# Filling TensorE's planned gaps with identity products during the first two attention units

## Chip, cores and metric

The kernel runs on one core of one Trainium2 chip. The metric is the device time of one execution in microseconds (us), from the first to the last thing that the core does. Lower is better.

## What is computed

Three stages follow one another. The first is an attention through packed queries: 32 packed queries per head attend to the 576 keys of their head, and the 576 true queries then attend to the 32 results. The second is a feed-forward layer with a gated activation. The third mixes 8 experts, whose weights per token come from a softmax that is normalised 8 times over rows and columns.

```python
p_packed = sm_attn(p, k, v)              # 4 batches, 8 heads, 32 packed queries, 64 wide
x = sm_attn(q, p_packed, p_packed)       # 2304 tokens x 512
h = x @ w_in; g = h * clip(h + 3, 0, 6) / 6; x = g @ w_out
P = softmax-like(x @ w_gate), normalised 8 times
out = sum over e of P[:, e] * (relu(x @ w1[e]) @ w2[e])
```

## The kernel before, in words

The attention is cut into 8 units `u` (a batch and four of its heads each), written by `attention(u, p_sb)`. A unit loads k, the packed queries p, q and v by DMA, and then on TensorE (PE): transposes k (L553, twelve transposes into `kT`), transposes the packed queries (L570), multiplies them with `kT` (L595, the first scores), transposes q (L643, nine), transposes the exponentials (L663, six), multiplies with v (L679), transposes the result (L704), multiplies with the transposed q (L736, the second scores), and transposes the second exponentials (L794, L798). Between these steps ScalarE (ACT), VectorE (DVE) and GpSimd (POOL) copy results out of PSUM, take maxima, exponentials and sums. The buffers of k, q, v and `kT` are single, so the DMA of a unit's k waits until the unit before has transposed its own.

Beside the attention, the feed-forward weights, which come as 64-bit floats, are decoded by integer and float operations on ACT, DVE and POOL (`split_f64`, L344 to L369) into `w1f` and others. Then the dense layers follow (L837, L886 to L888, L924 to L926, then L992 to L994 and L1050 to L1052), which start as soon as their operands are there.

The order is made by a planner, the class `Order`. Every operation is entered with an engine, a cost in microseconds, the buffers that it reads, writes or takes, and a priority. `run` keeps a clock per engine and again and again picks the open operation with the earliest planned start; what is picked is issued at once, by calling its function. The engines then work in that order, each strictly through its own queue, and the real waits are semaphores. The planned times decide the order alone. The costs that matter below are these:

```python
SYNC = 0.2                                            # added between an operation and what follows on it
def dma(kib, fn, **kw):                               # queue SP
    return order.op([("SP", max(0.6, kib / 350.0), fn)], lat=2.0, **kw)
pe(0.25, trans, reads=[kp[g]], writes=[ps], ...)      # three transposes of k, L553; four such steps in a unit
pe(0.55, scores, ...)                                 # half of the first scores, L595
pe(0.11 * n, trans, reads=[qp], ...)                  # n transposes of q, L643
pe(1.55, packed, ...)                                 # L679
pe(0.15 * len(tiles), scores, ...)                    # second scores, L736; 9 tiles in two steps
```

The queue SP is planned to issue two pieces of weights (512 KB each), four pieces of k (entered with 288), the first packed queries (64), four pieces of q (288) and v (576), in this order, and then the next pieces of weights and the next unit's k. `psum("po")` gives a bank of 128x512 floats; the two banks of that tag are used by the dense layers (L924 onward), not by the attention. `ident` is the 128x128 identity in 32-bit floats, made by POOL at the start.

Of the kernel before, what the change touches and what calls it, by code (L numbers as in the profile page):

```python
# [27 lines left out]
class Res:  # L28


    def __init__(self, count):
        self.free_at = [0.0] * count
# [31 lines left out]
class Order:  # L64
# [2 lines left out]

    def __init__(self):
        self.open, self.clock, self.all = [], {}, []

    def op(self, ways, reads=(), writes=(), fills=(), takes=(), after=(), prio=0, lat=0.0):
        deps = set(after)
        for h in (*reads, *writes):
            deps.update(h.writers)
        for h in writes:
            deps.update(h.readers)
        holds = list(dict.fromkeys((*reads, *writes, *fills, *takes)))
        for h in holds:
            h.users += 1
        o = Op(ways, holds, deps, (prio, len(self.all)), lat)  # L80
        self.all.append(o)
        for h in reads:
            h.readers.append(o)
        for h in (*writes, *fills):
            h.writers.append(o)
        if not o.wait:
            self.open.append(o)
        return o

    def run(self):  # L90
        while self.open:
            best = None
            for o in self.open:
                at, asked = o.ready, {}
                for h in o.holds:
                    if h.slot is None:
                        asked[h.res] = asked.get(h.res, 0) + 1
                for r, n in asked.items():
                    free = sorted(r.free_at)
                    at = max(at, free[n - 1] if len(free) >= n else float("inf"))  # L100
                _, start, eng, cost, fn = min(
                    (
                        (max(at, self.clock.get(w[0], 0.0)) + sum(w[3:], w[1]), max(at, self.clock.get(w[0], 0.0)), *w[:3])
                        for w in o.ways
                    ),
                    key=lambda w: w[0],
                )
                key = (start + PATIENCE * (o.lat == 0 and (o.prio[0] >= 100 or 9 < o.prio[0] < 20 and o.prio[0] % 1 > 0.3)), o.prio)
                if best is None or key < best[0]:
                    best = (key, start, o, eng, cost, fn)  # L110
            _, start, o, eng, cost, fn = best
            assert start < float("inf"), "no operation can go on"
            for h in o.holds:
                if h.slot is None:
                    h.slot = min(range(len(h.res.free_at)), key=lambda i: h.res.free_at[i])
                    h.res.free_at[h.slot] = float("inf")
                    h.t = h.make(h.slot)
            self.clock[eng] = self.now = start + cost
            fn()
            self.open.remove(o)  # L120
            o.end = start + cost + o.lat
            for h in o.holds:
                h.users -= 1
                h.last = max(h.last, o.end)
                if h.users == 0:
                    h.res.free_at[h.slot] = h.last + SYNC
            for a in o.after:
                a.wait.discard(o)
                a.ready = max(a.ready, o.end + SYNC)
                if not a.wait:  # L130
                    self.open.append(a)
# [19 lines left out]
def tile_kernel(  # L151
# [16 lines left out]
    nc = tc.nc  # L168
# [4 lines left out]
    E, _, F2 = moe2_w1.shape  # L173
# [82 lines left out]
    ident = const.tile([128, 128], F32, name="ident")  # L256
# [6 lines left out]
    order = Order()  # L263

    def maker(tag, shape, dt, parts):
        def make(i):
            r = res[tag]
            pool = r.pool if i < r.first else r.late_pool if i < r.first + r.late or not r.late else r.last_pool
            got = [pool.tile(shape, dt, tag=f"{tag}{x}_{i}", name=f"{tag}{x}_{i}") for x in parts]
            return got if len(parts) > 1 else got[0]  # L270

        return make

    def hold(tag, shape, dt=F32):
        return Hold(res[tag], maker(tag, shape, dt, ("",)))
# [544 lines left out]
    def psum(tag):  # L820
        return hold(tag, [128, 512])
# [381 lines left out]
    def early(gg):  # L1203

        return (9.4, 9.4, 13.4, 14.4, 100, 100, 100, 100)[gg]

    with tc.manual_schedule():
        nc.vector.memset(ones, 1.0)
        nc.vector.memset(three, 3.0)
        nc.vector.memset(maskb, 0.0)  # L1210
        nc.vector.memset(maskb[0:64, 0, :], 1.0)
        nc.vector.memset(maskb[64:128, 1, :], 1.0)
        nc.vector.memset(maskz, 0.0)
        for g in range(2):
            for h in range(2):
                r0 = 64 * g + 32 * h
                nc.vector.memset(maskz[r0:r0 + 32, g, h, :], 1.0)

        place("p0", att, 1)
        place("p1", att, 1)  # L1220
        p_sb = hold("p0", [128, 1, D]), hold("p1", [128, NU - 1, D])
        for u in range(NU):
            attention(u, p_sb)
        ws, pws = {}, {}

        def weights(gg):
            prio, soon = early(gg), gg < 4
            ws[gg] = (
                whole(gg, "w1", prio, "w1f", soon),
                whole(gg, "w2", prio + 0.5, ("w2", "w2o")[gg % 2], soon),  # L1230
            )

        for gg in range(4):
            weights(gg)
        order.op([("", 0.0, second_phase)], after=order.all)

        gps(0.2, lambda: nc.gpsimd.memset(wg.t, 0.0), writes=[wg], prio=90)
        dma(
            16,
            lambda: nc.sync.dma_start(wg.t[:, :, :E], moe2_w_gate.rearrange("(c p) e -> p c e", p=128)),  # L1240
            writes=[wg], prio=90,
        )
        begun = len(order.all)
        for i, (blk, g) in enumerate(units):
            batches = [span[0] for span in spans(blk)]
            for gg in (2 * g, 2 * g + 1):
                if gg not in ws:
                    weights(gg)
            for b in batches:
                if (b, 2 * g) not in pws:  # L1250
                    ggs = (2 * g, 2 * g + 1)
                    for some in [ggs] if i >= TOGETHER else [ggs[:1], ggs[1:]]:
                        pws.update(zip(((b, gg) for gg in some), packed_weights(i, b, [ws[gg][0] for gg in some])))
            hs = [pair("hs", [128, NFC, TB]) for _ in range(2)]
            for f in range(2 * NFC):
                layer1a(i, blk, f, {b: pws[b, 2 * g + f // NFC] for b in batches}, hs[f // NFC])
            layer2a(i, g, blk, [ws[2 * g][1], ws[2 * g + 1][1]], hs)
        uses = [[o for o in order.all[begun:] if a2[b] in o.holds] for b in range(B)]
        freed = []
        for b, count in enumerate((1, 2, 1, 2)):  # L1260
            freed = [order.op([("", 0.0, first_operands(count))], after=[*uses[b], *freed])]
        order.op([("", 0.0, third_phase)], after=order.all[begun:])
        for blk in range(NB):
            gate(blk)
        ops = {0: operands(0, 40)}
        routing()
        i = len(units)
        turn, done = 100 + G1, []
        for ps in passes:
            for pr in ps:  # L1270
                if pr not in ops:
                    ops[pr] = operands(
                        pr, 45 if pr > 1 else 200, lambda n, pr=pr: [done[-1] if pr > 1 else done[4 + 3 * n]]
                    )
            gs = list(range(G1, len(groups)))
            turns_of = [(gs[:2], pr) for pr in ps] + [([g], pr) for g in gs[2:] for pr in ps]
            ready = {}
            for some, pr in turns_of:
                for g in some:
                    if g not in ready:  # L1280
                        ready[g] = (*combined(g, turn), whole(g, "w2", turn, "w2"))
                        turn += 1
                for g in some:
                    wa, wb, w2 = ready[g]
                    hs = [pair("hs", [128, NFC, TB]) for _ in range(2)]
                    done.append(layer1b(i, ops[pr], wa, wb, hs))
                    for h in range(2):
                        layer2b(i, g, 2 * pr + h, w2, hs[h])
                    i += 1
        order.run()  # L1290
# [32 lines left out]
```

## Time and profile before

| | us |
|---|---|
| median of 3 runs | 1956.97 (1956.45 to 1958.83) |
| the profiled execution | 1956.3 |
| its span, first to last instruction | 1954.5 |
| TensorE busy in the span | 1917.1 |
| VectorE, ScalarE, GpSimd busy | 1216.6, 971.5, 887.5 |

The profile's times count from the first instruction of the span. The profiled execution lasts 1.8 us longer than its span and is 0.7 us under the median of the runs. A matrix product is two instructions, a load of the stationary operand (PEld) and a stream of the moving one (PE); the two rows overlap. A product of 32-bit floats that is not a transpose is issued as two such pairs. In a line of the timeline the columns are start, duration from the first start to the last end, engine, line of the code, operation, tiles written and read, shape, how many instructions, and in brackets the idle time of the engine before them with what ended it. "PEclk" is the clock that TensorE was granted as a share of 2.4 GHz, as far as the profile recorded it.

### The profile page before, as it was taken

The page shows a single profiled execution, that of the slowest core. Times are in us where ns is not written, and L with a number is a line of the kernel's source. Part 1 is how long each engine was busy: PE and PEld are TensorE (multiplying, and loading weights), DVE is VectorE, ACT ScalarE, POOL GpSimd, SP SyncE. Part 2 cuts the span into 40 slices and gives each one's busy share as a digit, 9 for nine tenths or more (in the row PEclk, how much of TensorE's full clock was granted, in tenths as well). Part 3 has the DMA queues.
Part 4 walks back from the last instruction along what each step waited for, and adds up shares of the span by engine and source line. Part 5 has one row for each costly group of instructions (what it writes and reads, how often), then busy time and mean ns, then how long its engine had stood idle before and what let it go on. Part 6 is the DMA issues. An engine that isn't in the chain of part 4 may idle for free.

```text
span 1954.5 us, 28065 instructions
## 1 busy us (share of the span) xinstructions
PE 1917.1 (98%) x10573; PEld 1736.5 (89%) x10573; DVE 1216.6 (62%) x2010; ACT 971.5 (50%) x2185; POOL 887.5 (45%) x925
## 2 busy tenths in 40 slices
PE   6999999999999999999999999999999999999998
PEld 4789999998899999999899999999999999999997
DVE  6996686447876766666745655555555555555554
ACT  6885674335455555555654443444444344444432
POOL 2445675246755666555633533334343342433321
PEclk9999999999999999999999999999999999999999
DMA  9831121001222222222311101111010111101102
GB/s 212 190 91 33 53 67 44 11 1 44 66 65 73 68 66 67 74 65 66 86 33 32 44 22 44 33 33 41 25 44 24 42 33 33 44 22 44 33 12 65
DMA packets 103544, 104.85 MB, mean 54 GB/s; under 512 B 42736, under 2 KB 78576, under 8 KB 103408
## 3 DMA queue, kind: packets, MB, share of 16 engines
q1 hardware_dynamic: 103408, 103.06, 19.2%
q8 instruction: 83, 1.36, 0.3%
q14 instruction: 53, 0.43, 0.1%
HBM read 98.32 MB, written 4.72 MB: 53 GB/s over the span
## 4 chain that ended last, share of the span: by engine, by line
PE 89%; DVE 7%; ACT 2%; issue 1%; POOL 0%; DMA 0%; SPq 0%; DVEq 0%; ACTq 0%; POOLq 0%
PE po L1052 13%; PE po L1051 13%; PE po L1050 13%; PE ph L992 12%; PE ph L994 12%; PE ph L993 12%; PE po L924 3%; PE po L926 3%; PE po L925 3%; PE ph L886 2%; PE ph L888 1%; PE ph L887 1%; PE ph L837 1%; DVE m_early L344 0%; DVE tmp L904 0%
## 5 line engine op out<-in xcount | busy, mean ns | idle before, releaser
L429 POOL TENSOR_TENSOR hsl<-tmp,hsh 128x384 fp32r<-128x384 f32 x382 | 389.9, 1028 | 812.1 <-PE ph L994 482.4
L1074 DVE SCALAR_TENSOR_TENSOR acc<-po,Pr,acc 128x512 f32<-128x512 f32 x504 | 372.4, 747 | 286.4 <-PE po L1052 285.9
L1052 PE MATMUL po<-w2h,hsl 128*128 128x512 f32 x1152 | 448.7, 389 | 0.3 <-DVE hsl L429 0.3
L1050 PE MATMUL po<-w2h,hsh 128*128 128x512 f32 x1152 | 449.0, 390 | 0.0
L1051 PE MATMUL po<-w2l,hsh 128*128 128x512 f32 x1152 | 448.7, 390 | 0.0
L300 ACT ACTIVATE tmp<-ph 128x384 f32<-128x384 f32 x291 | 141.4, 486 | 402.7 <-PE ph L994 401.1
L1006 DVE TENSOR_TENSOR tmp<-ph,tmp 128x384 f32<-128x384 f32 x288 | 159.2, 553 | 270.9 <-PE ph L994 184.2
L1052 PEld LDWEIGHTS po<-w2h,hsl 128*128 128x128 f32 x1152 | 216.2, 188 | 45.9 <-DVE hsl L429 0.8
L1050 PEld LDWEIGHTS po<-w2h,hsh 128*128 128x128 f32 x1152 | 216.3, 188 | 41.6
L1051 PEld LDWEIGHTS po<-w2l,hsh 128*128 128x128 f32 x1152 | 216.3, 188 | 41.6
L424 ACT ACTIVATE hsh<-tmp 128x384 fp32r<-128x384 f32 x480 | 239.3, 519 | 18.5 <-DVE tmp L904 12.5
L424 ACT ACTIVATE w2h<-raw 128x1024 fp32r<-128x1024 f32 x64 | 68.1, 1064 | 327.2 <-PE po L1052 315.1
L1014 ACT ACTIVATE tmp<-tmp 128x384 f32<-128x384 f32 x288 | 149.8, 520 | 36.2 <-DVE tmp L1006 29.5
L429 POOL TENSOR_TENSOR w1l<-raw,w1h 128x512 fp32r<-128x512 f32 (+1 forms) x124 | 157.2, 1268 | 0.2 <-ACT w1h L424 0.2
L992 PE MATMUL ph<-ax,w1h 128*128 128x384 f32 x448 | 151.2, 338 | 0.6 <-DVE tmp L301 0.6
L994 PE MATMUL ph<-ax,w1l 128*128 128x384 f32 x448 | 150.7, 336 | 0.0
L993 PE MATMUL ph<-ax,w1h 128*128 128x384 f32 x448 | 150.5, 336 | 0.0
L992 PE MATMUL ph<-xyh,w1h 128*128 128x384 f32 x320 | 108.1, 338 | 3.0 <-ACT tmp L300 3.0
L994 PE MATMUL ph<-xyh,w1l 128*128 128x384 f32 x320 | 108.0, 338 | 0.0
L993 PE MATMUL ph<-xyl,w1h 128*128 128x384 f32 x320 | 107.9, 337 | 0.0
L994 PE MATMUL ph<-ax,w1xl 128*128 128x384 f32 x320 | 107.8, 337 | 0.0
L992 PE MATMUL ph<-ax,w1xh 128*128 128x384 f32 x320 | 107.7, 337 | 0.0
(205 smaller groups left out, 3905.6 us busy)
## 6 DMA issues: line engine op xcount, KB each, us to landing
raw<-in_moe_w_dram SPq DMA_DIRECT2D x128, 512.0 KB, 3.5
raw<-in_moe_w_in_dram SPq DMA_DIRECT2D x16, 512.0 KB, 3.9
raw<-in_moe_w_out_dram SPq DMA_DIRECT2D x16, 512.0 KB, 3.6
k<-in_k_dram SPq DMA_DIRECT2D x32, 144.0 KB, 5.8
q<-in_q_dram SPq DMA_DIRECT2D x32, 144.0 KB, 4.6
v<-in_v_dram SPq DMA_DIRECT2D x8, 576.0 KB, 6.6
out_dram<-acc SPq DMA_DIRECT2D x36, 128.0 KB, 2.3
p<-in_p_dram SPq DMA_DIRECT2D x1, 224.0 KB, 5.4
```

The lines of the kernel that those rows point to most:

```text
L300: ("ACT", t_act(n, True), lambda: nc.scalar.activation(dst(), src(), AF.Copy)),
L424: t_act(n), lambda: nc.scalar.activation(dst(w.t[0]), src(), AF.Copy),
L429: lambda e: e.tensor_tensor(dst(w.t[1]), src(), as_f32(dst(w.t[0])), ALU.subtract),
L992: nc.tensor.matmul(out, wh[:, at + c, :], bh[:, c, :], start=first and c == 0, **on)
L993: nc.tensor.matmul(out, wh[:, at + c, :], bl[:, c, :], start=False, **on)
L994: nc.tensor.matmul(out, wl[:, at + c, :], bh[:, c, :], start=False, **on)
L1006: t_dve(n), lambda: nc.vector.tensor_tensor(u.t, ps.t[:, :n], u.t, ALU.add),
L1014: t_act(n, bool(ps)), lambda: nc.scalar.activation(c.t, src(), AF.Relu),
L1050: nc.tensor.matmul(ps.t, hh[:, f, ts], wh[:, f, :], start=(f == 0), stop=False)
L1051: nc.tensor.matmul(ps.t, hh[:, f, ts], wl[:, f, :], start=False, stop=False)
L1052: nc.tensor.matmul(ps.t, hl[:, f, ts], wh[:, f, :], start=False, stop=(f == NFC - 1))
L1074: lambda row=row, share=share, ps=ps: nc.vector.scalar_tensor_tensor(row(), ps.t, share(), row(), ALU.mult, ALU.add),
```

## The change

The planner gets a hook `fill`. While it is set, each time that the planner picks an operation for TensorE it first calls the hook with the planned gap (the planned start less the end of the operation before on TensorE). The hook issues `int(0.65 * gap / 0.12)` products of the identity with the first 64 columns of the identity into a bank `po` that nobody reads. The hook is set by an operation without engine at the very start and taken out by another one, which comes after all operations of unit 1; between them the bank is held. No clock or cost of the planner is changed by the hook.

```diff
     def __init__(self):
         self.open, self.clock, self.all = [], {}, []
+        self.fill = None
...
+            if eng == "PE" and self.fill:
+                self.fill(start - self.clock.get(eng, 0.0))
             self.clock[eng] = self.now = start + cost
             fn()
...
+        spare = psum("po")
+
+        def fill(gap):
+            for _ in range(int(0.65 * gap / 0.12)):
+                nc.tensor.matmul(spare.t[:, :64], ident, ident[:, :64], start=True, stop=True)
+
+        def begin():
+            order.fill = fill
+
+        def end():
+            order.fill = None
+
+        order.op([("", 0.0, begin)], takes=[spare], prio=0)
         for u in range(NU):
             attention(u, p_sb)
+            if u == 1:
+                order.op([("", 0.0, end)], takes=[spare], after=[o for o in order.all if o.prio[0] == 10 + u])
```

## Rows read from the trace of the kernel before

**Rows 1.** The page, busy tenths in 40 slices of the span: TensorE, its granted clock

```profile
PE   6999999999999999999999999999999999999998
PEclk9999999999999999999999999999999999999999
```

**Rows 2.** Busy time by stretches; columns: stretch, its length, engines' busy us, clock, DMA

```profile
0.00:7.80 7.80, 0.00 (x0) 0.02 (x1) 2.55 (x14) 4.36 (x7) 0.70 (x6) 1.00 0.85 212
7.80:24.00 16.20, 11.51 (x81) 8.05 (x83) 11.28 (x24) 9.73 (x25) 2.82 (x4) 1.00 1.20 224
24.00:46.00 22.00, 17.65 (x204) 12.80 (x200) 17.51 (x56) 15.85 (x47) 9.27 (x12) 1.00 0.91 198
46.00:150.00 104.00, 97.74 (x917) 84.30 (x914) 94.25 (x226) 85.97 (x214) 46.96 (x42) 1.00 0.61 139
```

**Rows 3.** Timeline of TensorE, unit 0

```profile
7.81 1.19 PE L553 MATMUL tp<-ident,k 96*128 96x96 f32 x6 [7.81 <-DMA k<-in_k_dram]
9.68 1.19 PE L553 MATMUL tp<-ident,k 96*128 96x96 f32 x6 [0.67 <-DMA k<-in_k_dram]
11.66 0.48 PE L570 MATMUL tp<-ident,pd 128*128 128x128 f32 x1 [0.80 <-POOL pd L539]
13.99 2.19 PE L595 MATMUL tp<-kT,pt 128*64 128x288 f32 x8 [1.85 <-DVE pt L575]
16.10 2.28 PE L643 MATMUL tp<-ident,q 128*128 128x128 f32 x9
18.39 1.13 PE L663 MATMUL tp<-ident,a 128*96 128x128 f32 x6
...
23.69 1.27 PE L736 MATMUL tp<-ppT,qT 128*64 128x64 f32 x36 [1.08 <-ACT ppT L300]
```

**Rows 4.** Timeline of TensorE, the same shapes in later units

```profile
26.45 1.19 PE L595 MATMUL tp<-kT,pt 128*64 128x288 f32 x8 [0.21 <-DVE pt L575]
...
33.98 0.71 PE L553 MATMUL tp<-ident,k 96*128 96x96 f32 x6
...
57.46 0.82 PE L663 MATMUL tp<-ident,a 128*96 128x128 f32 x6
...
67.08 1.25 PE L643 MATMUL tp<-ident,q 128*128 128x128 f32 x9 [0.62 <-ACT a L620]
```

**Rows 5.** Timeline of TensorE and its loads, products with 128 stationary columns

```profile
90.73 0.27 PE L886 MATMUL ph<-ax,pwh 128*128 128x192 f32 x1
90.84 0.27 PE L887 MATMUL ph<-ax,pwh 128*128 128x192 f32 x1
...
464.40 0.28 PE L1180 MATMUL ph<-cs,ones 128*128 128x8 f32 x2
...
464.17 0.42 PEld L1180 LDWEIGHTS ph<-cs,ones 128*128 128x128 f32 x2
```

**Rows 6.** Timeline of the other engines and of queue SP, unit 0

```profile
1.01 0.29 POOL masks.py:199 TENSOR_SCALAR_AFFINE_SELECT ident<-ident 128x128 f32<-128x128 f32 x1
9.35 0.62 ACT L367 ACTIVATE m_early<-m_early 128x512 f32<-128x512 f32 x1
11.20 2.87 SPq L388 DMA_DIRECT2D raw<-in_moe_w_in_dram  x2
12.95 0.69 DVE L344 TENSOR_TENSOR w1f<-m_early,raw 128x512 f32<-128x512 f32 x1
13.56 0.28 DVE L575 TENSOR_TENSOR pt<-tp,maskb 128x128 f32<-128x128 f32 x1
14.17 3.19 SPq L506 DMA_DIRECT2D k<-in_k_dram  x4
```

**Rows 7.** Timeline of VectorE and GpSimd, while unit 1 ends

```profile
36.02 0.46 DVE L605 TENSOR_REDUCE m<-tp 128x1 f32<-128x288 f32 x1 [1.03 <-PE tp L595]
...
36.89 1.30 POOL L344 TENSOR_TENSOR m_early<-raw,m_early 128x512 f32<-128x512 f32 x1 [3.90 <-DVE m_early L369]
```

**Rows 8.** The chain of work that ended last: start, us, what

```profile
16.17 1.06 PE tp L643 x4
```

## The prediction

> **What bounds the kernel now.** I read the page's slices first: TensorE is busy nearly everywhere but in the first slice, and its clock column reads full [rows 1]. The busy time by stretches then shows where TensorE stands still near the change: 7.80 us before its first instruction, 16.20 less 11.51 = 4.69 us up to the second scores of unit 0, 22.00 less 17.65 = 4.35 us until unit 1 is done, and 6.26 us in the next 104 us [rows 2]. The first 46 us thus hold 16.8 us of idle time; of them 1.4 can't be filled, as the identity is finished at 1.30 [rows 6]. Third, the timeline of unit 0 set beside later units: six transposes of k take 1.19 us against 0.71 later, the first scores 2.19 against 1.19, nine transposes of q 2.28 against 1.25, six of L663 1.13 against 0.82 [rows 3, 4]. Near twice the time for the same shapes is the lower of the two clocks, 1.2 GHz against 2.4. The clock column reads full there all the same [rows 1], so I trust the durations. TensorE stood idle before and between its first three bursts, and the clock rises only within L663, after work without a break since 13.99. The low clock costs 2 x 0.48 + 1.00 + 1.03 + 0.31 = 3.3 us, and part of it is on the chain that ends last [rows 8]. That is nearly all that the change can win: 0.17% of the time. A measurement of this kernel can tell about 0.2%, 3.9 us, from no change.
>
> **What the change adds: how many products.** The planned gaps follow from the planner's costs. Before the first transpose SP is planned to issue two pieces of weights (1.463 each) and two of k (0.823 each), 4.571; with 2.0 of latency and 0.2 of SYNC the step starts at 6.771, so int(0.65 x 6.771 / 0.12) = 36 products. The second pair of k is due at 6.217 + 2.2 = 8.417, after two steps that end at 7.271: a gap of 1.146, 6 products. The packed queries land at 9.017, their copy (planned 0.55) ends at 9.567, L570 starts at 9.767 after 8.917: 4 more (8 if POOL is late with the decode before it). For the rest I add up costs roughly: a unit costs TensorE 7.5 planned us, steps of units 2 and 3 and of L837 add some 7, unit 1 is planned to end near 38.5 (its loads are issued from 14.7 to 24.2), so some 8 us of gaps remain, with the cut to whole products some 35; step by step I get up to 55. I take 45, of them 27 in unit 0. In all **about 90 products**, bounds 70 and 130.
>
> **What one product costs.** The trace has no product of this shape. It is two loads of 128 columns with two streams of 64. Nearest rows: products with 128 stationary and 192 moving columns follow each other after 0.11 us at the high clock, and the pair with 128 stationary and 8 moving columns has its two streams done in 0.28 us, its two loads in 0.42 [rows 5]. A load of 0.2 us, and yet one product every 0.11: loads run beside the streams before them, and since 8 and 192 moving columns both stay near 0.11 to 0.14, the load sets the pace: 0.22 us for a product, nearly twice the 0.12 that the hook assumes. From below, the second scores, with 64 stationary and 64 moving columns, do 36 in 1.27: 0.035 each, 0.07 for two [rows 3]. From above, the two loads in a row, 0.42. I take 0.22 as the stationary width is the same, and 1.9 times as much, 0.42, while the clock is low. The Trainium skill ("TensorE: Matmul & The Clock Gate", Part 3, on what overlaps) says that a load overlaps with running products only where it goes to other row groups; here every load covers all rows, so by it load and stream would follow one another. This trace disagrees, by the 0.11 above; what the rule would make of the time is among the rivals.
>
> **The first gap.** The products can start at 1.4. In the kernel before, the clock rose some 4.5 us after unbroken work began; so I let it rise near 6. Until then 4.6 / 0.42 = 11 products, the other 25 at 0.22 take 5.5: the burst ends at 11.5. The first k is there at 7.81 [rows 3], and the transposes queue behind the burst on TensorE: **3.7 us late**.
>
> **The rest of unit 0.** Behind the late transposes stand the copies of `kT` on ACT, and in ACT's order behind them the decode step at 9.35; that feeds DVE's decode, which ends with `w1f` at 12.95 and stands ahead of `pt` [rows 6]. So DVE's part is moved too, by up to 3.7 us; I take 2.5. SP has the second piece of weights waiting for `w1f`, and unit 1's k behind it: 14.17 becomes some 16.7 [rows 6]. TensorE from 11.5 to the second scores has 37 products, 8.1 us, and its own steps, 11.51 less 3.3 = 8.2 us [rows 2]; without any wait the second scores start at 27.8, and as the tails of steps and products overlap, I take 27.2, against 23.69 [rows 3]: 3.5 us late, the 3.3 us of clock already counted.
>
> **Unit 1.** Some 18 products (28 at most), 4.0 to 6.2 us, fall into 4.35 us of idle time [rows 2]; but some of that idle has gone, as TensorE is later than its inputs, and what is left isn't where the planner had its gaps. I put 2 us on this. TensorE is thus **5.5 us late** when unit 1 ends.
>
> **What of it reaches the end.** Near 36 DVE waits 1.03 us for TensorE's scores, and GpSimd's decode waits for DVE [rows 7]: the lateness goes over into the decode. From 46 to 150 TensorE has 6.26 us idle and DVE 9.75 [rows 2]; both are late, so mostly the same waits come later. I let a tenth be made up: +5.0 us. Later TensorE is busy nearly throughout [rows 1], so nothing takes it back. Nothing else moves: the planner's times don't know of the products, the order of all other instructions stays, and the bank `po` is first wanted long after unit 1. Against the profiled execution's 1956.3 the sum is 1961.3; it stands 0.7 under the median, so I predict **1962**.
>
> **Rivals.** *The products are cheap.* If the load hides and only the 64 columns count (0.07, as the second scores suggest), the first burst is over before k lands. The point is 0.117 us a product: then 4.6 us at the low clock and 1.8 at the high, 4.6 / (1.9 x 0.117) + 1.8 / 0.117 = 36, end just at 7.81. Under it the clock is high from the start and nothing is late: 1957 less at most 3.3, some 1954. Against it speak the two pairs of rows with 128 stationary columns. Chance 0.14.
>
> *The lateness is made up.* Of 6.26 us idle from 46 to 150 and DVE's 9.75, most could vanish if the decode runs ahead: 5.5 shrinks to about 1.5, 1958.5. For it: the decode hardly needs TensorE. Against it: in-order queues that mix decode and attention, and rows 7 show them wait. Chance 0.22.
>
> *The products don't raise the clock.* The three short bursts before 13.99 did not raise it either [rows 3]. Then 36 products at 0.42 last 15.1 us, the first transpose starts at 16.5, 8.7 late, and the rise comes only with the scores: with 2 in unit 1, 10.7 late, nine tenths of it 9.6: 1966.5. Against it: work without a break did raise it, and the burst has no break. Chance 0.09.
>
> *Loads and streams follow one another*, the skill's rule. Then a product costs 0.42 + 0.07 = 0.49: the first burst has 5 products at the low clock and 31 at 0.49, ends at 21.2 and is 13.4 late; the other 54 cost 0.27 more each, 14.6, on top of the 1.8 above; nine tenths of 29.8 give 1984. Rows 5 speak against it. Chance 0.02.
>
> *It does next to nothing*: fewer gaps than I count, or products that only take idle time. Then 1957. Chance 0.03.
>
> **How the numbers follow.** The forecast has 0.50; its own range, from 70 to 130 products and 0.19 to 0.25 us each, is about 1959 to 1968, of which 0.43 is slower by over 0.2% (above 1960.9) and 0.07 within. The made-up case gives 0.20 within and 0.02 slower; cheap products 0.09 within and 0.05 faster; the low clock 0.09 and loads in a row 0.02 slower; nothing 0.03 within. Sums: faster 0.05, same 0.39, slower 0.56. For 8 in 10 I leave out the lower half of the cheap case, the loads in a row and the far end of the count: 1954.5 to 1968.5.
>
> **What would show it.** Right: in the timeline TensorE starts near 1.4 with some 72 instructions on the identity, about 0.2 us apart and then 0.11; the first transposes of k start near 11.5 and take 0.7, the scores 1.2; the second scores of unit 0 start near 27; SP's second piece of weights goes out later. In the stretch up to 46 TensorE is almost solidly busy, and idle time from 46 to 150 stays near 6. Wrong: transposes at 7.8 with instructions 0.06 apart (cheap); the first at 16 and the scores still at 2.2 (low clock); idle from 46 to 150 shrunk by 4 or more (made up); or an end that is over 3.9 us earlier, for which I see no source.

## The result, and the profile after

The changed kernel takes 1970.08 us (median of 6 runs, 1969.16 to 1971.31) against 1957.2 for the kernel before on the same chips: ratio 1.0066, 95% interval 1.0056 to 1.0076, so 12.9 us slower. The forecast was slower by 5.0, with 1968.5 as the upper end: the direction was right, the size was not, and the range missed it.

The lines of the changed code stand 3 higher from L344 on (L553 is L556, L595 is L598, L643 is L646, L736 is L739). The products of the change are L1231. First the page after, in the same slices as [rows 1] (its span is 1967.4 us, against 1954.5):

```profile
PE   9899999999999999999999999999999999999998
...
PEclk9999999999999999999999999999999999999999
```

TensorE's first slice is full now, and the clock column reads full as before. The timeline of TensorE says otherwise; it answers to [rows 3]:

```profile
1.36 15.62 PE L1231 MATMUL po<-ident 128*128 128x64 f32 x72 [1.36 <-POOL ident masks.py:199]
16.77 1.17 PE L556 MATMUL tp<-ident,k 96*128 96x96 f32 x6
17.73 2.71 PE L1231 MATMUL po<-ident 128*128 128x64 f32 x12
20.23 1.17 PE L556 MATMUL tp<-ident,k 96*128 96x96 f32 x6
21.20 4.00 PE L1231 MATMUL po<-ident 128*128 128x64 f32 x18
24.98 0.42 PE L573 MATMUL tp<-ident,pd 128*128 128x128 f32 x1
25.20 1.81 PE L1231 MATMUL po<-ident 128*128 128x64 f32 x8
26.93 2.19 PE L598 MATMUL tp<-kT,pt 128*64 128x288 f32 x8
29.05 1.69 PE L646 MATMUL tp<-ident,q 128*128 128x128 f32 x8
...
32.58 1.23 PE L1231 MATMUL po<-ident 128*128 128x64 f32 x10
...
37.32 1.27 PE L739 MATMUL tp<-ppT,qT 128*64 128x64 f32 x36
```

Read the durations, not the starts, first. 72 instructions (36 products) take 15.62 us, 0.43 a product. The transposes behind them still take 1.17 for six and the scores 2.19 for eight, as in the kernel before: the clock is at its lower level, 1.2 GHz, after 16 us without a break. It rises only in the transposes of q that follow the scores (eight in 1.69). Behind them ten instructions take 1.23, 0.24 a product. So 55 of the 86 products (110 of 172 instructions) are paid at the lower clock, all of them ahead of the scores. The scores start at 26.93 instead of 13.99, 12.9 late; the second scores at 37.32 instead of 23.69, 13.6 late.

What the lateness does to the other engines, ACT, DVE and queue SP (as [rows 6]):

```profile
17.49 0.89 ACT L303 ACTIVATE kT<-tp 128x288 f32<-128x288 f32 x2 [8.87 <-PE tp L556]
...
20.85 0.69 DVE L347 TENSOR_TENSOR w1f<-m_early,raw 128x512 f32<-128x512 f32 x1
25.44 0.29 DVE L578 TENSOR_TENSOR pt<-tp,maskb 128x128 f32<-128x128 f32 x1 [3.90 <-PE tp L573]
...
11.06 10.92 SPq L391 DMA_DIRECT2D raw<-in_moe_w_in_dram  x2
22.07 2.88 SPq L509 DMA_DIRECT2D k<-in_k_dram  x4
```

ACT stands 8.87 us before it can copy `kT`; the decode behind it, `w1f`, is 7.9 late (20.85 against 12.95), and with it unit 1's k (22.07 against 14.17). And the stretches (as [rows 2]; the last one begins 14 us after its counterpart):

```profile
7.80:24.00 16.20, 16.20 (x82) 16.20 (x81) 4.28 (x8) 2.99 (x7) 1.51 (x2) 1.00 0.64 124
...
60.00:164.00 104.00, 97.73 (x917) 84.13 (x912) 94.33 (x226) 85.78 (x214) 46.93 (x42) 1.00 0.64 139
```

From 7.8 to 24 TensorE is never idle, while DVE falls from 11.28 us of work to 4.28. And from 60 on the changed kernel repeats what the other did from 46 on: 917 instructions and 97.73 us in 104, against 917 and 97.74 [rows 2]. The whole program is moved by 14 us there, and 12.9 of it is left at the end of the span.

### The profile page after: what moved, and what is told of

It reads as the page before. It is cut to its first block, busy times and chain, and to the rows that moved or that the text cites. A ratio compares the mean times of both kernels' runs of the same rounds, so it can differ in the third digit from the quotient of the medians.

```text
span 1967.4 us, 28409 instructions
## 1 busy us (share of the span) xinstructions
PE 1944.2 (99%) x10745; PEld 1765.6 (90%) x10745; DVE 1215.3 (62%) x2010; ACT 971.8 (49%) x2185; POOL 887.0 (45%) x925
## 4 chain that ended last, share of the span: by engine, by line
PE 91%; DVE 6%; ACT 2%; issue 0%; DMA 0%; POOL 0%; DVEq 0%; POOLq 0%; ACTq 0%; SPq 0%
PE po L1055 13%; PE po L1054 13%; PE po L1053 13%; PE ph L995 12%; PE ph L997 12%; PE ph L996 12%; PE po L927 3%; PE po L929 3%; PE po L928 3%; PE ph L889 2%; PE ph L891 1%; PE ph L890 1%; PE po L1231 1%; PE ph L840 1%; DVE tmp L907 0%
```

## The experiments

Theory: the products run at the lower clock and don't raise it, so 55 of them at 0.43 us stand ahead of the scores, where less than 10 us were idle; their price and number is the whole loss. Rivals: the loss comes from elsewhere (order, later gaps); it is the values (an identity is nearly all zeros) that leave the clock low; and, once the clock was in doubt, that a full clock would win or lose nothing here. Ratios are to the kernel before, run on the same chip.

**Wider products** (1978.35 us, ratio 1.0115, 1.010 to 1.013).

```diff
-                nc.tensor.matmul(spare.t[:, :64], ident, ident[:, :64], start=True, stop=True)
+                nc.tensor.matmul(
+                    spare.t[:, :256], ident, maskz.rearrange("p g h d -> p (g h d)"), start=True, stop=True
+                )
```

> Same products, same number, but the moving operand is a 256-column tile of zeros and ones instead of 64 columns of the identity. At the lower clock 256 columns take about as long as the load of 128 (0.21 us), so the price at the lower clock stays near 0.43 a product. Theory A (what the products stream decides whether the clock rises, 64 columns beside a load of 128 were too little): the clock rises during the first burst, which then ends near 12 instead of 17.0; the first scores take about 1.2 instead of 2.19, and the time falls by 5 to 8 us, to 1962 to 1965. Theory B (products on the identity or on constants never raise it, whatever their width): first transposes near 17 again, scores 2.2, time 1970.

Its timeline of TensorE, and after it the groups by line from 3 to 7.5 and from 8 to 20 us:

```profile
2.54 18.72 PE L1231 MATMUL po<-maskz,ident 128*128 128x256 f32 x72 [2.54 <-DVE maskz L1220]
21.10 0.66 PE L556 MATMUL tp<-ident,k 96*128 96x96 f32 x6
...
30.55 1.19 PE L598 MATMUL tp<-kT,pt 128*64 128x288 f32 x8
```

```profile
L1231 PE MATMUL po<-maskz,ident 128*128 128x256 f32 x12 | 5.5, 645 | 2.5 <-DVE maskz L1220 2.5
...
L1231 PE MATMUL po<-maskz,ident 128*128 128x256 f32 x55 | 12.4, 386 | 0.0
```

The clock rises inside the first burst: the mean duration of one instruction, which overlaps with the next, falls from 645 to 386 ns, the transposes take 0.66 and the scores 1.19. On the clock theory A is right. On the time I was wrong: 256 columns are not free beside the load. At the lower clock 12 instructions take 5.5 us (0.92 a product), at the full one 55 take 12.4 (0.45), so 72 of them still need 18.7 us, and the kernel is slower than the change.

**Ones for the identity** (1970.73 us, 1.0075, 1.006 to 1.009).

```diff
-                nc.tensor.matmul(spare.t[:, :64], ident, ident[:, :64], start=True, stop=True)
+                nc.tensor.matmul(spare.t[:, :64], ones, ones[:, :64], start=True, stop=True)
```

> Same shapes and number as the change, but both operands are ones instead of the identity, which is nearly all zeros. Theory A (shape decides): no difference, first transposes near 16.8, scores 2.2, time 1970. Theory B (the values decide, zeros do not wake the clock): the clock rises in the first burst, first transposes near 11 to 12, scores 1.2, time near 1963.

```profile
1.05 15.62 PE L1231 MATMUL po<-ones 128*128 128x64 f32 x72 [1.05 <-DVE ones L1211]
...
26.63 2.19 PE L598 MATMUL tp<-kT,pt 128*64 128x288 f32 x8
```

Up to the scores the timeline is the change's, with the same durations: the zeros of the identity are not what leaves the clock low.

**Without the first burst** (1962.15 us, 1.0028, 1.0016 to 1.0039) and **the first burst alone** (1964.12 us, 1.0045, 1.003 to 1.006; the same edit with `== 0.0`).

```diff
-            if eng == "PE" and self.fill:
+            if eng == "PE" and self.fill and self.clock.get(eng, 0.0) > 0.0:
```

> The change without the products before the first transposes (36 of its 86). If the loss is the price of 0.43 for each of the 55 products ahead of the scores, less the waits that they cover: first transposes at 7.8, the other 19 products take 8.2 us against 3.3 us of waits before the scores, so the scores start near 18.5 instead of 13.99 and the time is 1961 to 1963. If the loss is the first burst alone: 1957. If the lateness is made in the later gaps: 1968 or more.

> The change with the products before the first transposes alone (36 of its 86). By the price at the lower clock: first transposes at 16.8, 9 us late; the waits of 0.67, 0.80 and 1.85 us ahead of the scores then vanish in part, as loads and decode are ready earlier than TensorE, so the scores start 6.5 to 8.5 us late and the time is 1963 to 1965. If nearly all of the change's 12.9 us came from the first burst: 1969.

TensorE without the first burst, then with it alone:

```profile
7.90 1.19 PE L556 MATMUL tp<-ident,k 96*128 96x96 f32 x6 [7.90 <-DMA k<-in_k_dram]
8.89 2.72 PE L1231 MATMUL po<-ident 128*128 128x64 f32 x12
...
18.10 2.19 PE L598 MATMUL tp<-kT,pt 128*64 128x288 f32 x8
```

```profile
1.36 15.62 PE L1231 MATMUL po<-ident 128*128 128x64 f32 x72 [1.36 <-POOL ident masks.py:199]
16.77 2.13 PE L556 MATMUL tp<-ident,k 96*128 96x96 f32 x12
...
21.89 2.19 PE L598 MATMUL tp<-kT,pt 128*64 128x288 f32 x8 [2.78 <-DVE pt L578]
```

Both came out as the price says: scores 4.1 and 7.9 us late, the kernel 6.0 and 7.9 us slower by the medians (5.5 and 8.8 by the ratios). Without the first burst, the products behind the scores cost a little more: the second scores, at 29.11, are 5.4 late. The two halves together make 13.9 (14.3), about the change's 12.9; each half has an interval of over 2 us either way, and within that nothing is left for another place.

**The number fitted to the price** (1957.20 us, 1.0000, 0.9991 to 1.0010): one identity product for every 0.5 us instead of every 0.12.

```diff
-            for _ in range(int(0.65 * gap / 0.12)):
+            for _ in range(int(0.65 * gap / 0.5)):
```

> The change's identity products, one for every 0.5 us instead of one for every 0.12, so 8 before the first transposes and about 18 in all. At 0.43 each the first burst ends at 4.9, ahead of k; the clock stays low. If the loss was price times number: first transposes at 7.8, scores 2.2, time within 1 us of before. If the products harm in another way (order, semaphores, the bank): several us slower.

```profile
1.36 3.68 PE L1231 MATMUL po<-ident 128*128 128x64 f32 x16 [1.36 <-POOL ident masks.py:199]
7.72 1.19 PE L556 MATMUL tp<-ident,k 96*128 96x96 f32 x6 [2.69 <-DMA k<-in_k_dram]
...
13.72 2.19 PE L598 MATMUL tp<-kT,pt 128*64 128x288 f32 x8 [1.53 <-DVE pt L578]
```

Eight products end at 5, TensorE waits for k again, and the time is that of the kernel before. Neither the bank nor the hook costs anything that this run can show; its interval is about 2 us either way.

**Wide products, fitted** (1957.20 us, 1.0000, 0.9991 to 1.0009): 256 columns of ones, one for every 0.5 us; and **the first eight of them alone** (1956.82 us, 0.9999, 0.9990 to 1.0008), with the condition of the first-burst run.

```diff
-            for _ in range(int(0.65 * gap / 0.12)):
-                nc.tensor.matmul(spare.t[:, :64], ident, ident[:, :64], start=True, stop=True)
+            for _ in range(int(0.65 * gap / 0.5)):
+                nc.tensor.matmul(
+                    spare.t[:, :256], ones, ones[:, None, :].to_broadcast([128, 2, 128]), start=True, stop=True
+                )
```

> Products with 256 moving columns (all ones), as the 256-column run showed them to raise the clock, but one for every 0.5 us of 0.65 of the gap instead of one for every 0.12, so 8 before the first transposes. At 0.92 a product at the lower clock and 0.46 at the full one they end at 7 to 8.2. Theory A (the loss was the lower clock and the number): first transposes at 7.8 to 8.3 and at full speed (0.7), scores 1.2, second scores of unit 0 two to three us earlier than 23.69, time 1953.5 to 1956. Theory B (the lower clock before the scores is off the path, so raising it gains nothing): 1956 to 1957.

> The 8 wide products before the first transposes alone, nothing in the later gaps. If the clock, once raised, holds through the waits of 0.67, 0.80 and 1.85 us: as the fitted wide run, 1953.5 to 1956. If it falls in those waits: first transposes at 0.7 but scores at 2.2, time 1956 to 1957.

The fitted run: TensorE's timeline with one line of queue SP, and one line of its chain of work that ended last, from 22 to 50 us:

```profile
7.66 0.69 PE L556 MATMUL tp<-ident,k 96*128 96x96 f32 x6 [1.01 <-DMA k<-in_k_dram]
...
13.74 1.19 PE L598 MATMUL tp<-kT,pt 128*64 128x288 f32 x8 [1.56 <-DVE pt L578]
...
22.00 1.27 PE L739 MATMUL tp<-ppT,qT 128*64 128x64 f32 x36 [0.61 <-ACT ppT L303]
...
26.64 1.49 SPq L509 DMA_DIRECT2D k<-in_k_dram  x2
...
34.88 0.69 PE L556 MATMUL tp<-ident,k 96*128 96x96 f32 x6 [1.43 <-DMA k<-in_k_dram]
...
36.26 1.26 PE L739 MATMUL tp<-ppT,qT 128*64 128x64 f32 x35
```

```profile
26.20 12.58 DMA raw<-in_moe_w_out_dram x2
```

The kernel before, queue SP and the second scores of unit 1:

```profile
28.32 2.24 SPq L506 DMA_DIRECT2D k<-in_k_dram  x2
...
35.69 1.28 PE L736 MATMUL tp<-ppT,qT 128*64 128x64 f32 x35
```

The first eight alone, and a stretch of it in the columns of [rows 2]:

```profile
7.53 0.69 PE L556 MATMUL tp<-ident,k 96*128 96x96 f32 x6 [0.61 <-DMA k<-in_k_dram]
...
13.62 2.19 PE L598 MATMUL tp<-kT,pt 128*64 128x288 f32 x8 [2.00 <-DVE pt L578]
```

```profile
15.00:18.00 3.00, 3.00 (x13) 1.75 (x9) 1.28 (x4) 1.10 (x4) 0.00 (x0) 0.50 1.13 329
```

In the fitted run the change does what a full clock can do: transposes 0.69, scores 1.19, second scores 1.7 us earlier than in the kernel before (22.00 against 23.69). And the time does not move, to within the 1.8 us of the interval. The eight alone raise the clock too, but it has fallen again by the scores (2.19), after the waits between the bursts; and that run takes no longer. In it the clock column does show the lower level, 0.50 from 15 to 18 us, behind the rise in the burst; in the other timelines shown here the lower level lies ahead of the first rise, and the column reads full there. Fast or slow clock ahead of the scores, three runs (the two fitted ones and this one) end within 0.4 us of one another. Where the 1.7 us go can be read in the trace of the fitted run. The second half of unit 2's k is issued 1.7 us earlier than in the kernel before (26.64 against 28.32), but while unit 1 ends TensorE waits 1.43 for it at 34.88, where it hardly waited before [rows 4]. The second scores of unit 1 start at 36.26, later than the 35.69 of the kernel before, and the chain stands 12.58 us on a load of weights. The products did not use up the gain, as only one of them (0.60 us, at 27.65) lies between 22 and 36 us. The loads set the pace there, not TensorE. That is read from waits and chain; a run with fewer loads was not made.

**Wide first, then the change's own products** (1957.17 us, 0.9999, 0.9991 to 1.0008): the eight wide products replace the 36 of the first gap, the other 50 stay.

```diff
+            if order.clock.get("PE", 0.0) == 0.0:
+                for _ in range(int(0.65 * gap / 0.5)):
+                    nc.tensor.matmul(
+                        spare.t[:, :256], ones, ones[:, None, :].to_broadcast([128, 2, 128]), start=True, stop=True
+                    )
+                return
             for _ in range(int(0.65 * gap / 0.12)):
```

> The 8 wide products before the first transposes, and from there on the change's own 50 identity products in the later gaps. If the step that failed in the prediction is the clock alone: the identity products now cost about 0.23 each as they do behind the scores, the 19 ahead of the scores 4.4 us, the scores start at 13.5 to 15 and take 1.2, time 1955 to 1959. If the clock falls again during the identity products: they cost 0.43, the scores start near 18 and take 2.2, time 1962, as in the run without the first burst.

```profile
8.39 1.48 PE L1237 MATMUL po<-ident 128*128 128x64 f32 x12
...
10.30 2.09 PEld L1237 LDWEIGHTS po<-ident 128*128 128x128 f32 x18
10.38 2.15 PE L1237 MATMUL po<-ident 128*128 128x64 f32 x18
...
14.08 1.19 PE L598 MATMUL tp<-kT,pt 128*64 128x288 f32 x8 [0.60 <-DVE pt L578]
```

The same 12 and 18 instructions that took 2.72 and 3.99 us now take 1.48 and 2.15, the scores start on time, and 50 products cost nothing that the interval (1.8 us either way) can show. Beside the run without the first burst, which has the same 50 products, 19 of them at the lower clock, and is 6.0 us slower than the kernel before, this shows the clock's share by itself.

**The forecast's own picture** (1959.53 us, 1.0014, 1.0005 to 1.0023): wide products first, then 16 identity products at the full clock, meant to end where the forecast had the first burst end, then the 50. And **23 identity products in the first gap alone** (1959.31 us, 1.0014, 1.0005 to 1.0023).

```diff
+            count = int(0.65 * gap / 0.12)
+            if order.clock.get("PE", 0.0) == 0.0:
+                ...
+                count = 16
-            for _ in range(int(0.65 * gap / 0.12)):
+            for _ in range(count):
```

> The forecast's own picture, made to happen: 8 wide products raise the clock, 16 identity products at the full clock then carry the first burst to 11 to 11.5, and the later gaps have the change's 50 identity products. If the rest of the prediction's sum is right, and only the clock was wrong: second scores of unit 0 near 27, time 1961 to 1962. If the loads of unit 1 hide what is left of the lateness, as they hid the gain of the full clock: 1957 to 1959.5.

> 23 identity products before the first transposes at the lower clock, and none later, so the first transposes start near 11.5, 3.7 late, against 9 late with 36 (7.9 us more in all). If lateness of the first transposes goes to the end one for one: plus 3.5. If the waits of 0.67, 0.80 and 1.85 ahead of the scores and the loads of unit 1 take up the first few us: plus 0.5 to 2.5.

The first of the two, TensorE:

```profile
6.67 3.68 PE L1238 MATMUL po<-ident 128*128 128x64 f32 x32
10.19 0.67 PE L556 MATMUL tp<-ident,k 96*128 96x96 f32 x6
...
24.40 1.27 PE L739 MATMUL tp<-ppT,qT 128*64 128x64 f32 x36
...
41.01 0.63 PE L646 MATMUL tp<-ident,q 128*128 128x128 f32 x4 [1.24 <-DMA q<-in_q_dram]
```

The second:

```profile
1.36 10.08 PE L1231 MATMUL po<-ident 128*128 128x64 f32 x46 [1.36 <-POOL ident masks.py:199]
11.23 2.13 PE L556 MATMUL tp<-ident,k 96*128 96x96 f32 x12
...
16.35 2.19 PE L598 MATMUL tp<-kT,pt 128*64 128x288 f32 x8 [2.78 <-DVE pt L578]
```

Both are 2.3 to 2.5 us slower than the kernel before, inside the second expectation of the second and at the upper edge of that of the first. In the first the burst ends at 10.19, 1.3 us before the forecast's 11.5; the second scores come at 24.40, not near 27 as I had it, and part of the products of unit 1 then fall into waits. In the second the transposes are 3.4 us late and the scores 2.4; with 36 products they were 9.0 and 7.9. So the waits ahead of the scores take up about a microsecond, and after the scores lateness passes on nearly whole.

## Why the prediction was right and wrong

**Right:** the direction; that the products are more than the gaps hold; their number (86 against "about 90": 36, 6, 9 and 4 ahead of the scores, where I had 36, 6, 4 and the 8 of the late decode as an aside); their price, 0.43 at the lower clock and 0.24 or less at the full one against 0.42 and 0.22; the way the lateness takes, through the copies of `kT` on ACT, the decode on DVE and SP's second piece of weights to unit 1's k; and that only a tenth would be made up (14.0 us at 60, 12.9 at the end).

**Wrong, the step that decides:** "I let it rise near 6". The clock did not rise in the first burst, nor in the 19 products behind it. That made the first transposes 9.0 late, not 3.7, and went on: the 55 products hold TensorE for 23.4 us ahead of the scores (15.41, 2.50, 3.78 and 1.73, from the start of each burst to the start of what follows). The idle time there was 6.45 us ahead of k (7.81 less 1.36) and waits of 0.67, 0.80 and 1.85 [rows 3], 9.8 in all; 13.6 are left, and the scores are 12.9 late, as the products also start into the tails of the transposes. I had drawn the rise from the work after 13.99 in the kernel before, as if any work without a break were the same. That work was products with 288 moving columns and then transposes with 128; the burst was 64 moving columns beside loads of 128. With 256 in their place the clock rose within the burst. Why the narrow ones leave it low, no run here shows. The rival "the products don't raise the clock" had this mechanism, at 0.09. Its 1966.5 was too low as well, as it paid only the 36 products at the lower clock, and not the 19 that follow ahead of the scores.

**Wrong in size, two terms behind it.** The full clock ahead of the scores was put at up to 3.3 us of gain; the fitted wide run had the full clock in all of these steps and won nothing that its interval can show, as TensorE then waits for loads while unit 1 ends. And with the clock up, as I assumed, the forecast's 5.0 measured 2.5: the second scores are 0.7 late instead of 3.5, of which 1.3 is the burst that ended sooner. The rival with cheap products likewise foresaw 1954 for products that fit, and the fitted ones gave 1957.

The rule of the Trainium skill ("TensorE: Matmul & The Clock Gate", Part 3, on what overlaps), that a load overlaps with running products only in other row groups, would have made 0.42 + 0.07 = 0.49 us of a product at the full clock. This case's traces disagree: the 64-column products keep 0.117 an instruction there, and the 18 loads and 18 streams of one burst take 2.09 and 2.15 us in the same stretch, so load and stream overlap, as the rows of before had it. The 256-column ones do not tell: their 0.45 a product may be stream alone, or stream and load in a row.

## What to carry to other kernels

Before filling idle time with dummy work, measure one filler in place, at the clock that it will meet, and see in the durations of the work behind it whether it raised that clock; a clock column that reads full is no proof, as here it read full through the whole 15.62 us of the first burst. A planned gap is no idle time: what of the fillers outlasts the real wait delays all that queues behind them. And make sure first that a faster clock in that place would shorten the whole: here no gain showed, even with fillers that raised the clock.

## What the runs showed of the hardware that I had not expected

- TensorE stayed at the lower clock through 72 instructions of 64 columns without a break (15.62 us), with an identity as with ones; with 256 columns and the same loads it rose within the burst, and eight such products before the first k were enough in four runs.
- A 32-bit float product of 128 stationary columns took 0.117 us an instruction with 64 moving columns and about 0.23 with 256 at the full clock (12.4 us for 55), 0.217 and 0.46 at the lower one. I had expected 256 columns to hide beside the load. The products with 192 columns in [rows 5], one every 0.11 us, don't price them: their operands have another 32-bit type (fp32r in the code), and the trace has one pair of instructions for each such product, not two.
- A raised clock falls again in the waits of unit 0: transposes at 0.69 and scores at 2.19 in the run with the first eight alone, and a granted clock of 0.50 from 15 to 18 us.
